# Fourier mixing and a squared-ReLU layer: a cosine table by permutation, another fold order for the first batch, and stores by group at the end

## The chip, the cores and the metric

The kernel runs on one core of a Trainium2 chip. The metric is device time in microseconds (us) of one execution; where one number stands for several executions it is their median. The profiled execution is one of its own, with a time of its own.

## What is computed

The reference, cut to what matters (x is 8 x 3008 x 256, w_in 256 x 2048, w_out 2048 x 256, all float32):

```python
X = np.fft.fft(np.fft.fft(x, axis=1), axis=2).real      # 3008 along the sequence, 256 along the features
t = X.reshape(24064, 256)
h = np.maximum(t @ w_in, 0.0)
out = (h * h) @ w_out                                   # 24064 x 256, float32
```

## The kernel before

**Method.** Only the real part of the two transforms is wanted, and it falls into cosine and sine products. Write C and S for the tables along the sequence, c and s for those along the features. The kernel computes Z = C x and Z' = S x on TensorE (matmuls in float16) with one column for each of half of the output rows. It multiplies c and s into w_in once, which gives `gh` (`gh_step`, L441 to L447: four pieces of 512 columns, two tables each; ACT, the ScalarE, scales them on the way out of PSUM). `gh` times Z and Z', summed, is t @ w_in for one sequence index k. A third product with the doubled, negated sine part (`gh_turn`, L449) turns this sum in place into that of the mirrored row S − k. So every column of Z serves two output rows.

**Folds.** x is folded before it is multiplied: along d (feature d with 256 − d) and along n (sequence place n with its mirrors), so that the odd frequencies need 752 places and the even ones fewer. For each batch: x comes in as four quarters of its rows, xo, 128 partitions x 6 rows x 256 (`load_x`, L116; plain and indirect DMAs that POOL, the GpSimd, issues and that make float16 of float32). DVE, the VectorE, folds in d (`d_even` L360, `d_odd` L364: 128 x 3072 elements each), then in n (`n_cos` L369, `n_sin` L372), then makes the odd class `od` (`odd` for one half, `odds` for both, L376 and L379) and the even class `ev` (`even`, L390). `nyq` (L381) moves one column of `od` with two permutation matmuls. The even class goes to a scratch DRAM tensor and back in another order (`scr`, `rb`, L392 to L406), and is folded again by `fold8` and `fold16` (L415, L426; the `late` steps). Batch 0 of the fold order is x[1]; x[0] comes last.

**Tables.** `table_steps` (L228) makes the sine and cosine tables by range reduction: `args` and `turns` round, `mods` gives the remainder m, `absm` |m| for the cosine, and ACT's Sin function does the rest (`sins`, `coss`, L270 to L280). For the odd class each table has six rows of 376 columns. `weigh` (L282) halves the rows' end places with the small vector `wgt`, which POOL makes (L202 to L207). The even class's table (e = 1) is made later, in window 2.

**Windows.** The 12,040 columns of Z are cut into 25 windows (`FIRST`, then 512 each; the last has 360). Units (i, e), fold number and class, hold some 752 columns each: (0, 0), (1, 0), (0, 1), (1, 1), then both classes of each batch in turn. Every window has eight stages (L694 to L705), and each stage has two of 16 blocks of 128 hidden features:

- `pq`: four matmuls into PSUM (L666, L667).
- `square`: ReLU on ACT (L676), square on DVE (L678).
- `others`: the fold or table steps of this stage (`at`, `post`), an eighth of the second product of the previous window (`ffn2_steps`, matmuls L587), and from stage `lo` to `hi` the Z products of the units that begin in the next window (`z_steps`, L461).
- `turn`: two matmuls (L672), then `square` again for the mirrored rows.

Window 0 takes its stages in pairs. A Z product of a unit has two parts (0 cosine, 1 sine). Each is made in two halves: the first goes through ACT into `es` (L486), the second stays in PSUM, ACT copies it to `zc` or `zs` (L490), and `minus` (L497) gets the other columns as 2 es − PSUM on DVE.

**Second product.** `part` (L580) sums 16 matmuls for each group of 128 output rows. Two groups share a PSUM tile; then ACT copies both at once into `osb` (L593; in the last window the pieces are 128 x 512 and 128 x 256), and SP, the SyncE, issues the stores (L569), one for each run of rows with an even step.

**What sets the order.** `tc.manual_schedule()` (L98): the program text is the order on each engine. Each engine runs its own queue in order and waits on semaphores for the others. Ahead of window 0, L531 to L552 set it: `weigh`, the folds, the Z products of unit (0, 0), all four `gh_step`s, `minus` (jobs `z0(0, 2)`, `z0(1, 2)`) and all `gh_turn`s. 28 matmuls of zeros on the tile `spn` (L327) stand ahead of these on PE, the TensorE.

The functions that the change touches, and their callers:

Of the kernel before, what the change touches and what calls it, by code (L numbers as in the profile page):

```python
# [14 lines left out]
HS = 32.0  # L15
# [13 lines left out]
def kernel(  # L29
# [136 lines left out]
    evec_i = iota([P, 2], [[1, 2]], 0, 2, "evec_i")  # L166
    dvec_i = iota([P, 2], [[P, 2]], 0, 1, "dvec_i")
    xs = {0: load_x(0, idx_first)}
    w16 = const.tile([P, 2, F], F16, name="w16")
    nc.gpsimd.dma_start(out=w16, in_=moe_w_in.rearrange("(c p) f -> p c f", p=P))  # L170
    wout16 = const.tile([P, NFC, D], F16, name="wout16")
    nc.gpsimd.dma_start(out=wout16, in_=moe_w_out.rearrange("(c p) o -> p c o", p=P))
    prow_i = iota([P, P], [[1, P]], 0, 1, "prow_i")
    idx["c"] = iota([P, 1], [[1, 1]], P - 1, -1, "idx_c")
# [21 lines left out]
    phase = small([P, R], "phase")  # L196
    nc.gpsimd.tensor_scalar(out=phase, in0=nraw, scalar1=0.0, scalar2=float(math.pi / 2), op0=ALU.is_ge, op1=ALU.mult)
    wg0 = small([P, R], "wg0")
    nc.gpsimd.tensor_scalar(out=wg0, in0=nraw, scalar1=float(Q), scalar2=None, op0=ALU.is_le)
    nc.gpsimd.tensor_tensor(phase, phase, wg0, op=ALU.mult)  # L200

    wgt = small([P, R], "wgt")  # L202
    wg1 = small([P, R], "wg1")
    nc.gpsimd.tensor_scalar(out=wgt, in0=nraw, scalar1=0.0, scalar2=-0.5, op0=ALU.is_equal, op1=ALU.mult)
    nc.gpsimd.tensor_scalar(out=wg1, in0=nraw, scalar1=float(Q), scalar2=-0.5, op0=ALU.is_equal, op1=ALU.mult)
    nc.gpsimd.tensor_tensor(wgt, wgt, wg1, op=ALU.add)
    nc.gpsimd.tensor_scalar(out=wgt, in0=wgt, scalar1=1.0, scalar2=None, op0=ALU.add)  # L207


    perm = [const.tile([P, P], F16, name=f"perm{i}") for i in range(2)]  # L210
    for i in range(2):
        nc.gpsimd.tensor_scalar(out=perm[i], in0=prow_i, scalar1=float(P - 1 - i), scalar2=None, op0=ALU.is_equal)
# [15 lines left out]
    def table_steps(e):  # L228
# [44 lines left out]
        def coss(h):  # L273
            if e:
                nc.scalar.activation(cos_t, st["t", h][:, 0:nr, 0:n], AF.Sin, bias=halfpi[:, 0:1], scale=-wk)
                return

            for j0, j1 in ((0, 1), (1, 2), (2, 3)) if h == 0 else ((0, 1), (1, 3)):
                r = RQ[3 * h + j0]
                nc.scalar.activation(cos_t[:, 3 * h + j0 : 3 * h + j1, :], st["t", h][:, j0:j1, 0:n], AF.Sin, bias=phase[:, r : r + 1], scale=-wk)  # L280

        def weigh():  # L282
            if e:
                for t in (cos_t, sin_t):
                    for r in range(2):
                        nc.vector.tensor_scalar(out=t[:, r, :], in0=t[:, r, :], scalar1=wge[:, r : r + 1], scalar2=None, op0=ALU.mult)
                return

            for t, r in ((cos_t, 5), (sin_t, 1)):
                q = RQ.index(r)  # L290
                nc.scalar.activation(t[:, q, :], t[:, q, :], AF.Copy, bias=0.0, scale=wgt[:, r : r + 1])
# [16 lines left out]
    for c in range(2):  # L308
        nc.vector.scalar_tensor_tensor(out=am[:, c, :], in0=drow, scalar=dvec[:, c : c + 1], in1=at[:, c, :], op0=ALU.mult, op1=ALU.add)
    to["args"](0)  # L310
# [10 lines left out]
    spn = fop.tile([P, 2, 2, P], F16, name="spn")  # L321
    to["turns"](0)
    to["mods"](0)
    nc.vector.memset(spn, 0.0)  # L324

    pw = ps_o.tile([P, 512], F32, name="pw", tag="po")
    for i in range(28):  # L327
        nc.tensor.matmul(pw[:, 0 : 3 * P], spn[:, 0, 0, :], spn.rearrange("p c r d -> p (c r d)")[:, 0 : 3 * P], start=True, stop=True)  # L328
    to["absm"](0)
    to["turns"](1)  # L330
    to["sins"](0)
    to["coss"](0)
    to["mods"](1)
    to["absm"](1)
    to["sins"](1)
    to["coss"](1)
    fe = fop.tile([P, 4, R, 130], F16, name="fe")
    fo = fop.tile([P, 4, R, 130], F16, name="fo")
    fo0 = fo.rearrange("p q c d -> p (q c) d")[:, :, 0:1]
    nc.vector.memset(bass.AP(tensor=fo0.tensor, offset=fo0.offset, ap=list(fo0.ap[0:2]) + [[129, 2]]), 0.0)  # L340
    nc.vector.memset(fe.rearrange("p q c d -> p (q c) d")[:, :, 129:130], 0.0)

    folded = {}

    def fold_steps(i):
        t = xs.pop(i)
        ab = fop.tile([P, 2, 2, R, 130], F16, name="ab", tag="ab")
# [7 lines left out]
        fef = fe.rearrange("p q c d -> p (q c) d")  # L355
        fof = fo.rearrange("p q c d -> p (q c) d")
# [17 lines left out]
        def odd(part):  # L374

            nc.vector.tensor_tensor(od[:, part, :, part:129], ab[:, part, 0, :, part:129], ab[:, part, 1, :, part:129], op=ALU.subtract)  # L376

# [10 lines left out]
        def even():  # L388

            nc.vector.tensor_tensor(ev.rearrange("p r c d -> p c r d"), ab[:, :, 0], ab[:, :, 1], op=ALU.add)  # L390
            scr = drp.tile([R * P, 260], F16, name="scr", tag="scr")
            nc.gpsimd.dma_start(out=scr.rearrange("(p r) d -> p (r d)", r=R), in_=ev.rearrange("p r c d -> p (r c d)"))  # L392
            st["scr"] = scr
# [15 lines left out]
        def fold8(sg):  # L409
            if sg == 0:  # L410
                xt = st["xt"] = fop.tile([P, 2, 2, 2, 260], F16, name="xt", tag="xt")
                yt = st["yt"] = fop.tile([P, 2, 2, 2, 130], F16, name="yt", tag="yt")
                folded[i, 1] = (xt, yt)
            rb = st["rb"]
            nc.vector.tensor_tensor(st["xt"][:, sg], rb[:, 0:2], rev_dim(rb[:, 2:4], 2), op=ALU.subtract if sg else ALU.add)  # L415
# [21 lines left out]
        return {"d_even": d_even, "n_cos": n_cos, "odd": odd, "odds": odds, "d_odd": d_odd, "n_sin": n_sin, "nyq": nyq, "even": even, "back": back, "late": late}  # L437
# [3 lines left out]
    def gh_step(cc):  # L441
        f0 = cc * 512
        pg = ps_h.tile([P, 2, 512], F32, name="pg", tag="psh")
        for i, t in enumerate((c_all, s_n)):
            for c in range(2):
                nc.tensor.matmul(pg[:, i, :], t[:, c, 0:P], w16[:, c, f0 : f0 + 512], start=(c == 0), stop=(c == 1))  # L446
        nc.scalar.activation(gh[:, 0:2, f0 : f0 + 512], pg, AF.Copy, bias=0.0, scale=1.0 / HS)  # L447
# [13 lines left out]
    def z_steps(u, late=False):  # L461
# [15 lines left out]
        def mm(part, h, k, last, o0, o1, lhs, tab):  # L477
            if h == 0 and k == 0:
                st[part] = ps_z.tile([P, 512], F32, name="pz", tag="pz")
            ps = st[part]  # L480
            nc.tensor.matmul(ps[:, o0:o1], lhs, tab, start=(h == 0 and k == 0), stop=last, skip_group_check=True)  # L481
            if not last:
                return
            if h == 0:
                es = st["es", part] = evp.tile([P, NE], F32, name="es", tag="es")
                nc.scalar.activation(es[:, 0:n], ps[:, 0:n], AF.Copy, bias=0.0, scale=1.0)  # L486
                return
            es = st["es", part]
            for w, o, a, cnt in spans(c0, n):
                nc.scalar.activation(zwin(w)[part][:, o : o + cnt], ps[:, a : a + cnt], AF.Copy, bias=0.0, scale=1.0)  # L490
            if not late:
                minus(part)

# [5 lines left out]
        def jobs(part, h):  # L499
            if h == 2:  # L500
                return [lambda: minus(part)]
# [25 lines left out]
    def run(*jobs):  # L527
        for j in jobs:
            j()
# [3 lines left out]
    to["weigh"]()  # L533
    run(f0s["d_even"], f0s["n_cos"], lambda: f0s["odd"](0))
    run(*z0(0, 0))
    run(f0s["d_odd"])
    gh_step(0)
    run(*z0(0, 1))
    run(f0s["n_sin"], lambda: f0s["odd"](1), f0s["nyq"])
    gh_step(1)  # L540
    gh_step(2)
    run(*z0(1, 0))
    run(*z0(1, 1))
    gh_step(3)
    run(*z0(0, 2))
    run(*z0(1, 2))

    turn2 = small([P, 1], "turn2")
    nc.vector.tensor_scalar(out=turn2, in0=dvec[:, 0:1], scalar1=0.0, scalar2=2.0, op0=ALU.is_equal, op1=ALU.mult)
    nc.vector.tensor_scalar(out=turn2, in0=turn2, scalar1=-2.0, scalar2=None, op0=ALU.add)  # L550
    for cc in range(F // 512):
        gh_turn(cc)  # L552

    def store(osb, p0, g0, m, minus):

        for b, k0, kstep, n, c0 in runs:
# [12 lines left out]
            nc.sync.dma_start(  # L569
# [3 lines left out]
    def ffn2_steps(w, h2):  # L573
# [6 lines left out]
        def part(i, hf):  # L580
# [7 lines left out]
            if hf == 1 and (j == 1 or i + 1 == len(groups)):  # L588
# [33 lines left out]
    for w in range(NW):  # L622
# [7 lines left out]
        if w == 0:  # L630
            at[2] = [f0s["even"], f0s["back"]]
        elif w == 1:
            fj = fold_jobs(1)
            at = [[f] for f in fj[0:5]] + [[], fj[6:7], []]
            post[5] = fj[5:6]
            lo, hi = 6, NST
        elif w == 2:
            te = table_steps(1)
            at = [[lambda: te["freq"](), lambda: te["args"](0)], [lambda: te["turns"](0)], [lambda: te["mods"](0)],
                  [lambda: te["absm"](0)], [lambda: te["sins"](0)], [lambda: te["coss"](0)], [], [lambda: te["weigh"]()]]  # L640
            for st in range(4):
                at[st + 3] = at[st + 3] + f0s["late"][st : st + 1]
            at[7].append(folds[1]["back"])
# [4 lines left out]
        elif w == win_of(col_of[1, 1]) - 1:  # L648
            for st in range(4):
                at[st] = folds[1]["late"][st : st + 1]  # L650
            lo = 4
# [55 lines left out]
    for j in ffn2_steps(*old):  # L707
        j()
# [30 lines left out]
```

## Time and profile before

| | |
|---|---|
| three runs | 640.37 us median (640.24 to 640.47) |
| the profiled execution | 640.28 us |
| its span in the trace | 638.4 us |
| PE busy | 615.2 us, 96% of the span |
| ACT busy | 459.4 us, 72% |
| DVE busy | 369.8 us, 58% |
| POOL busy | 79.9 us, 13% |
| moved by DMA | 47.52 MB |

PE is the bound, at nearly full load; the matmuls of the second product (L587) alone take 361.7 us. How to read it: the span is what the trace covers from the first to the last instruction, and the execution's own time is 1.9 us longer. Line numbers of the kernel before are written L587. A `window` of the kernel is one of the 25 stretches of columns; it is not a window of time. Times along the span are counted from its start.

### The profile page before, as it was taken

Reading aid. Unit: us, or ns where it says so; the run is one execution under the profiler, and the core shown is the slowest. Engines: PE = TensorE matmul, PEld = TensorE weight load, DVE = VectorE, ACT = ScalarE, POOL = GpSimd, SP = SyncE. Lnnn points to the kernel's source line nnn. Section 1 sums busy time; section 2 is a strip of 40 time slices with the busy share of each in tenths; the row PEclk is TensorE's granted clock in tenths of the full one; section 3 lists DMA queues with packets and bytes.
Section 4 is the critical chain, followed back from the end, with each engine's and each line's share of the span. In section 5 each row is a group of like instructions: output and inputs, shape, how many; then the busy total and the mean of one; then the engine's idle time right before and its main releaser. Section 6 shows DMA issues by size and latency. Waiting matters only on the chain.

```text
span 638.4 us, 11578 instructions
## 1 busy us (share of the span) xinstructions
PE 615.2 (96%) x4540; PEld 438.1 (69%) x4540; DVE 369.8 (58%) x604; ACT 459.4 (72%) x612; POOL 79.9 (13%) x131
## 2 busy tenths in 40 slices
PE   4789999999999999999999999999999999999995
PEld 2456796676776767776677767776777767777785
DVE  8786645775547557745576455854567545454440
ACT  7777767867777777767777777777777777776751
POOL 8450110022001300210011100130000200000000
PEclk9999999999999999999999999999999999999998
DMA  8935121072111711631117211262111311111112
GB/s 161 193 70 130 49 75 42 24 151 90 43 43 43 178 60 51 142 97 36 50 39 169 69 51 39 59 160 61 40 43 50 101 36 48 37 48 49 37 55 57
DMA packets 36268, 47.52 MB, mean 74 GB/s; under 512 B 4215, under 2 KB 30327, under 8 KB 36215
## 3 DMA queue, kind: packets, MB, share of 16 engines
q0 software_dynamic: 9072, 22.14, 17.0%
q1 hardware_dynamic: 27143, 24.65, 12.9%
q8 instruction: 35, 0.57, 0.4%
q14 instruction: 18, 0.15, 0.1%
HBM read 33.63 MB, written 27.84 MB: 96 GB/s over the span
## 4 chain that ended last, share of the span: by engine, by line
PE 90%; ACT 4%; DMA 2%; issue 2%; DVE 1%; POOL 1%; ACTq 0%; POOLq 0%
PE po L587 50%; PE ph L672 13%; PE ph L666 12%; PE ph L667 12%; PE pz L481 3%; ACT h L676 3%; DMA w<-in_moe_w_in_dram 2%; ACT gh L447 1%; DVE h L678 0%; POOL xo L130 0%; PE pg L446 0%; ACT osb L593 0%; DVE od L379 0%; POOL xo L125 0%; ACT zc L490 0%
## 5 line engine op out<-in xcount | busy, mean ns | idle before, releaser
L676 ACT ACTIVATE h<-ph 128x1024 f16<-128x1024 f32 (+3 forms) x400 | 368.4, 974 | 80.8 <-PE ph L672 77.4
L678 DVE TENSOR_TENSOR h<-h 128x1024 f16<-128x1024 f16 (+3 forms) x400 | 262.8, 660 | 233.4 <-ACT h L676 231.6
L587 PE MATMUL po<-wout,h 128*128 128x256 f16 (+1 forms) x3024 | 361.7, 273 | 0.0
L587 PEld LDWEIGHTS <-h 128*128 128x128 f16 (+1 forms) x3024 | 296.6, 98 | 71.5
L666 PE MATMUL ph<-zc,gh 128*128 128x512 f16 (+3 forms) x400 | 145.4, 366 | 1.2 <-ACT gh L447 0.7
L667 PE MATMUL ph<-zs,gh 128*128 128x512 f16 (+3 forms) x400 | 145.5, 366 | 0.1
L672 PE MATMUL ph<-zs,gh 128*128 128x512 f16 (+3 forms) x400 | 113.8, 366 | 4.6 <-ACT h L676 4.2
L593 ACT ACTIVATE osb<-po 128x512 f32<-128x512 f32 (+2 forms) x98 | 56.8, 584 | 68.2 <-PE po L587 63.4
L667 PEld LDWEIGHTS <-gh 128*128 128x128 f16 x400 | 39.1, 98 | 44.9 <-issue 2.8
L666 PEld LDWEIGHTS <-gh 128*128 128x128 f16 x400 | 39.0, 98 | 42.6 <-issue 0.4
L672 PEld LDWEIGHTS <-gh 128*128 128x128 f16 x400 | 37.0, 97 | 14.8 <-issue 8.0
L432 POOL COPY xt<-xt 128x2 f16<-128x2 f16 x16 | 2.5, 187 | 184.4 <-DVE xt L415 184.4
L130 POOL DMA_INDIRECT xo<-in_x_dram,idx_r x15 | 18.8, 1256 | 4.5 <-issue 4.3
L125 POOL DMA_DIRECT2D xo<-in_x_dram x8 | 6.1, 760 | 101.8 <-DVE fo L364 101.7
L402 POOL DMA_INDIRECT rb<-scr,idx_r x16 | 18.1, 1133 | 4.9 <-issue 4.9
L486 ACT ACTIVATE es<-pz 128x376 f32<-128x376 f32 (+1 forms) x32 | 15.4, 481 | 4.3 <-PE pz L481 4.2
L490 ACT ACTIVATE zs<-pz 128x376 f16<-128x376 f32 (+23 forms) x27 | 8.5, 359 | 10.8 <-PE pz L481 10.8
L328 PE MATMUL pw<-spn 128*128 128x384 f16 x28 | 7.3, 444 | 8.2 <-DVE spn L324 8.2
L497 DVE SCALAR_TENSOR_TENSOR zs<-es,pz 128x376 f16<-128x376 f32 (+22 forms) x27 | 9.4, 383 | 9.8 <-ACT zs L490 9.8
L360 DVE TENSOR_TENSOR fe<-xo 128x3072 f16<-128x3072 f16 x8 | 14.3, 1786 | 0.3
L364 DVE TENSOR_TENSOR fo<-xo 128x3072 f16<-128x3072 f16 x8 | 14.2, 1780 | 0.0
L497 DVE SCALAR_TENSOR_TENSOR zc<-es,pz 128x376 f16<-128x376 f32 (+22 forms) x27 | 9.4, 383 | 6.9 <-ACT zc L490 6.9
(108 smaller groups left out, 225.1 us busy)
## 6 DMA issues: line engine op xcount, KB each, us to landing
out_dram<-osb SPq DMA_DIRECT2D x77, 128.0 KB
xo<-in_x_dram POOLq DMA_DIRECT2D x7, 768.0 KB, 7.0
scr<-ev POOLq DMA_DIRECT2D x8, 390.0 KB, 4.1
rb<-scr POOLq DMA_DIRECT2D x16, 130.0 KB, 3.6
out_dram<-osb SPq DMA_DIRECT2D x12, 94.0 KB
w<-in_moe_w_in_dram POOLq DMA_DIRECT2D x1, 1024.0 KB, 11.9
wout<-in_moe_w_out_dram POOLq DMA_DIRECT2D x1, 1024.0 KB, 16.4
out_dram<-osb SPq DMA_DIRECT2D x8, 75.0 KB
```

The costliest lines, as they stand in the source:

```text
L130: nc.gpsimd.indirect_dma_start(out=flat(q), out_offset=None, in_=bass.AP(tensor=x.tensor, offset=0, ap=[[XW, B * S * D // XW], [1, XW]]), ...
L402: nc.gpsimd.indirect_dma_start(out=rb[:, q].rearrange("p r d -> p (r d)"), out_offset=None, in_=bass.AP(tensor=src.tensor, offset=src.offs ...
L481: nc.tensor.matmul(ps[:, o0:o1], lhs, tab, start=(h == 0 and k == 0), stop=last, skip_group_check=True)
L486: nc.scalar.activation(es[:, 0:n], ps[:, 0:n], AF.Copy, bias=0.0, scale=1.0)
L497: nc.vector.scalar_tensor_tensor(out=zwin(w)[part][:, o : o + cnt], in0=es[:, a : a + cnt], scalar=2.0, in1=ps[:, a : a + cnt], op0=ALU.mu ...
L587: nc.tensor.matmul(po[0:m, j * D : (j + 1) * D], h2[:, fc, q : q + m], wout16[:, fc, :], start=(fc == 0), stop=(fc == NFC - 1))
L593: nc.scalar.activation(osb[0:mm].rearrange("p s d -> p (s d)")[:, lo:hi], po[0:mm, lo:hi], AF.Copy, bias=0.0, scale=HS * HS)
L666: nc.tensor.matmul(ph[:, a, 0:wn], gh[:, 0, f0 : f0 + P], zcw[:, 0:wn], start=True, stop=False)
L667: nc.tensor.matmul(ph[:, a, 0:wn], gh[:, 1, f0 : f0 + P], zsw[:, 0:wn], start=False, stop=True)
L672: nc.tensor.matmul(phs[s][:, a, 0:wn], gh[:, 2, f0 : f0 + P], zsw[:, 0:wn], start=False, stop=True, skip_group_check=True)
L676: nc.scalar.activation(h1[:, :, 0:wn], phs[s][:, :, 0:wn], AF.Relu)
L678: nc.vector.tensor_tensor(h2[:, 2 * s : 2 * s + 2, sg * wn : (sg + 1) * wn], hv, hv, op=ALU.mult)
```

## The change

- **Cosine table (odd class).** The six rows of the cosine table are no longer computed by Sin from |m|. Each is a mirror image of a row of the sine table, so two matmuls with permutation matrices (`perm`) put two rows at a time into PSUM, and ACT copies them out (three copies of 128 x 752). `absm` for this table, its two Sin calls for six rows, and the vectors `phase` and `wg0` go; `wgt` shrinks to one column, and one weighing is left. POOL makes `perm` early. The 28 zero matmuls become 16 + 4 + 4 + 8, spread between these steps, and `spn` is cleared earlier.
- **Fold of batch 0.** It is folded in n first, on all 256 features, then in d: `u_odd` and `u_part` make the odd class; `v_even` and `v_part` make the even class later, in window 2. The next load of x is issued after `v_even`.
- **w_in** is loaded by two DMAs of half the columns. `gh` pieces 0 and 1 are made ahead of window 0 (0 scaled by ACT, 1 by DVE), piece 2 in stage 0 (ACT) and piece 3 in stage 2 (DVE) of window 0, into the PSUM tiles of the second product. `minus` of unit (0, 0), with ACT's copies of the columns of window 1 (`rest`), stands in stage 4 of window 0.
- **Windows 1 to 4.** The folds of batch 1, the even class's table, the `late` folds and the Z products are put into other stages.
- **The end.** In the last window each group of rows is copied and stored by itself; the odd groups' mirrored rows are stored through ACT's queue.

The diff, cut to its core:

```diff
-    w16 = const.tile([P, 2, F], F16, name="w16")
-    nc.gpsimd.dma_start(out=w16, in_=moe_w_in.rearrange("(c p) f -> p c f", p=P))
+    w16 = [const.tile([P, 2, F // 2], F16, name=f"w16_{i}") for i in range(2)]
+    for i in range(2):
+        nc.gpsimd.dma_start(out=w16[i], in_=moe_w_in[:, i * F // 2 : (i + 1) * F // 2].rearrange("(c p) f -> p c f", p=P))
...
+    for i in (1, 0):
+        nc.gpsimd.tensor_scalar(out=perm[i], in0=prow_i, scalar1=float(P - 1 - i), scalar2=None, op0=ALU.is_equal)
...
-    phase = small([P, R], "phase")
-    nc.gpsimd.tensor_scalar(out=phase, in0=nraw, scalar1=0.0, scalar2=float(math.pi / 2), op0=ALU.is_ge, op1=ALU.mult)
-    wg0 = small([P, R], "wg0")
-    nc.gpsimd.tensor_scalar(out=wg0, in0=nraw, scalar1=float(Q), scalar2=None, op0=ALU.is_le)
-    nc.gpsimd.tensor_tensor(phase, phase, wg0, op=ALU.mult)
-    wgt = small([P, R], "wgt")
...
+    wgt = small([P, 1], "wgt")
+    nc.gpsimd.tensor_scalar(out=wgt, in0=nraw[:, 1:2], scalar1=float(Q), scalar2=-0.5, op0=ALU.is_equal, op1=ALU.mult)
     nc.gpsimd.tensor_scalar(out=wgt, in0=wgt, scalar1=1.0, scalar2=None, op0=ALU.add)
...
         def coss(h):
...
+            pc = ps_h.tile([P, 2, 512], F32, name="pc", tag="psh")
+            for j in range(2):
+                r = RQ[2 * h + j]
+                nc.tensor.matmul(pc[:, j, 0:n], perm[1 if r else 0], sin_t[:, RQ.index(6 - r if r else 0), :], start=True, stop=True)
+            nc.scalar.activation(cos_t[:, 2 * h : 2 * h + 2, :], pc[:, :, 0:n], AF.Copy, bias=0.0, scale=1.0)
...
     to["turns"](0)
     to["mods"](0)
+    to["sins"](0)
     to["turns"](1)
+    to["weigh"]()
+    idle(4)
     to["coss"](0)
     to["mods"](1)
     to["sins"](1)
+    idle(4)
     to["coss"](1)
+    to["coss"](2)
+    idle(8)
...
+        def u_odd():
+            nc.vector.tensor_copy(t[0:1, 2, 0, :], t[0:1, 0, R - 1, :])
+            nc.vector.tensor_tensor(u, tq[:, :, 0], tq[:, :, 1], op=ALU.subtract)
+        def u_part(sg):
+            nc.vector.tensor_tensor(cs[:, sg], u[:, 0], rev_dim(u[:, 1], 1), op=ALU.subtract if sg else ALU.add)
+            d_fold(od[:, sg], cs[:, sg], sg)
+            if not sg:
+                nc.scalar.activation(od[:, 0, :, 0:1], cs[:, 0, :, 0:1], AF.Copy, bias=0.0, scale=1.0)
+        def v_even():
+            nc.vector.tensor_tensor(v, tq[:, :, 0], tq[:, :, 1], op=ALU.add)
+            xs[i + 1] = load_x(i + 1)
+        def v_part(sg):
+            w = fop.tile([P, R, D], F16, name="w", tag="ab")
+            nc.vector.tensor_tensor(w, v[:, 0], rev_dim(v[:, 1], 1), op=ALU.subtract if sg else ALU.add)
+            d_fold(ev[:, :, sg], w, sg)
...
+    def gh_scale(out, pg, act):
+        if act:
+            nc.scalar.activation(out, pg, AF.Copy, bias=0.0, scale=1.0 / HS)
+        else:
+            nc.vector.tensor_scalar(out=out, in0=pg, scalar1=1.0 / HS, scalar2=None, op0=ALU.mult)
+    def gh_step(cc, act, late=False):
...
+        pg = None if late else ps_h.tile([P, 2, 512], F32, name="pg", tag="psh")
+            pt = ps_o.tile([P, 512], F32, name="pg", tag="po") if late else pg[:, i, :]
...
+                if late and w > 0:
+                    continue
                 nc.scalar.activation(zwin(w)[part][:, o : o + cnt], ps[:, a : a + cnt], AF.Copy, bias=0.0, scale=1.0)
...
+        def rest(part):
+            for w, o, a, cnt in spans(c0, n):
+                if w > 0:
+                    nc.scalar.activation(zwin(w)[part][:, o : o + cnt], st[part][:, a : a + cnt], AF.Copy, bias=0.0, scale=1.0)
...
-                return [lambda: minus(part)]
+                return [lambda: minus(part), lambda: rest(part)]
...
-    to["weigh"]()
-    run(f0s["d_even"], f0s["n_cos"], lambda: f0s["odd"](0))
-    run(*z0(0, 0))
-    run(f0s["d_odd"])
-    gh_step(0)
-    run(*z0(0, 1))
-    run(f0s["n_sin"], lambda: f0s["odd"](1), f0s["nyq"])
-    gh_step(1)
-    gh_step(2)
-    run(*z0(1, 0))
-    run(*z0(1, 1))
-    gh_step(3)
-    run(*z0(0, 2))
-    run(*z0(1, 2))
-    for cc in range(F // 512):
-        gh_turn(cc)
+    run(f0s["u_odd"], lambda: f0s["u_part"](0))
+    run(*z0(0, 0))
+    gh_step(0, True)
+    run(lambda: f0s["u_part"](1), f0s["nyq"])
+    run(*z0(0, 1))
+    gh_step(1, False)
+    run(*z0(1, 0))
+    run(*z0(1, 1))
+    gh_turn(0)
+    gh_turn(1)
+    run(f0s["v_even"])
...
+            if hf == 1 and tail:
+                osb = osp.tile([P, 2, D], F32, name="osb", tag="osb")
+                nc.scalar.activation(osb[0:m, 0, :], po[0:m, j * D : (j + 1) * D], AF.Copy, bias=0.0, scale=HS * HS)
+                nu = max(0, min(m, wn - q))
+                if nu:
+                    store(osb[:, 0, :], 0, g0 + q, nu, False)
+                if nu < m:
+                    store(osb[:, 0, :], nu, g0 + 2 * wn - q - m, m - nu, True, nc.scalar if i % 2 else nc.sync)
...
         if w == 0:
-            at[2] = [f0s["even"], f0s["back"]]
+            at[0] = [lambda: gh_step(2, True, True), lambda: gh_turn(2)]
+            at[2] = [lambda: gh_step(3, False, True), lambda: gh_turn(3)]
+            at[4] = z0(0, 2) + z0(1, 2)
         elif w == 1:
-            at = [[f] for f in fj[0:5]] + [[], fj[6:7], []]
+            at = [[], fj[0:1], fj[1:2], fj[2:3], fj[3:5], [], [], []]
...
         elif w == 2:
...
-            at[7].append(folds[1]["back"])
+            at = [[folds[1]["even"]], [lambda: te["freq"](), lambda: te["args"](0)], [lambda: f0s["v_part"](0)], [lambda: f0s["v_part"](1), f0s["even"], f0s["back"]],
+                  [lambda: te["turns"](0)], [lambda: te["mods"](0)], [lambda: te["absm"](0), lambda: te["sins"](0)], [lambda: te["coss"](0)]]
+        elif w == 3:
+            at[0] = [lambda: te["weigh"]()]
+            for st in range(4):
+                at[1 + st // 2] = at[1 + st // 2] + f0s["late"][st : st + 1]
+            at[3] = [folds[1]["back"]]
+            lo, hi = 4, NST
...
         elif w == win_of(col_of[1, 1]) - 1:
             for st in range(4):
-                at[st] = folds[1]["late"][st : st + 1]
-            lo = 4
+                at[1 + st] = folds[1]["late"][st : st + 1]
+            lo, hi = 5, NST
...
-    for j in ffn2_steps(*old):
+    for j in ffn2_steps(*old, tail=True):
```

In the prediction, L561, L736 and L741 are lines of the changed kernel: L561 is the subtraction in `minus` (L497 before), L736 the second matmul of `pq` (L667 before) and L741 that of `turn` (L672 before).

## The prediction

> **What bounds the kernel now.** I read the 40 slices first, then the chain of waits of the first 60 us, then the timeline of each engine there and at the end.
>
> ```profile
> PE   4789999999999999999999999999999999999995
> PE 90%; ACT 4%; DMA 2%; issue 2%; DVE 1%; POOL 1%; ACTq 0%; POOLq 0%
> ```
>
> TensorE (PE) is full from slice 4 on and holds 90% of the chain. The change takes no matmul out of that part, so time can only be won or lost before PE is full (the first 55 us), where one window hands over to the next, and after the last matmul. Table by stage (us, then PE, PEld, DVE, ACT, POOL busy; the last row is the hand-over from window 3 to 4, where PE lacks 1.1 us):
>
> ```profile
> 15.00:20.00 5.00, 4.05 (x23) 1.84 (x22) 4.90 (x7) 2.25 (x5) 4.59 (x6) 1.00 1.32 197
> 20.00:25.00 5.00, 3.24 (x21) 1.84 (x19) 1.96 (x8) 3.96 (x7) 2.65 (x3) 1.00 1.19 182
> 30.00:35.00 5.00, 4.26 (x28) 2.51 (x26) 3.17 (x8) 4.36 (x8) 1.49 (x4) 1.00 0.29 101
> 100.00:110.00 10.00, 8.89 (x56) 5.27 (x55) 6.14 (x11) 7.95 (x10) 0.31 (x2) 1.00 0.08 26
> ```
>
> The chain there (start, us, what):
>
> ```profile
> 5.26 11.87 DMA w<-in_moe_w_in_dram
> 17.17 1.04 PE pg L446 x4
> 18.23 1.02 ACT gh L447
> 19.70 1.87 ACT gh L447 x2
> 21.99 0.64 PE pz L481 x3
> 23.53 1.03 ACT gh L447
> ```
>
> Window 0 waits for w_in and then for ScalarE (ACT), which copies four gh pieces between the z copies. Its first ReLU starts at 24.45, window 1's first matmul at 33.10 and window 2's at 55.31. The end:
>
> ```profile
> 628.64 4.38 SPq L569 DMA_DIRECT2D out_dram<-osb  x8
> 631.56 0.65 ACT L593 ACTIVATE osb<-po 128x256 f32<-128x256 f32 x2 [2.95 <-PE po L587]
> SPq L734 <- DMA out_dram<-osb: 3.4, 1, 3.4
> ```
>
> The last matmul ends at 631.49, the last store is issued by 633.02, SP then waits 3.4 us for stores to land (636.5), and 1.9 us close the span at 638.4. The profiled execution took 640.28 against a median of 640.37 (640.24 to 640.47), so I add to 640.28.
>
> **Part 1, up to window 0's first ReLU: 3.4 us earlier.** GpSimd (POOL) now makes both perms before wgt. By starts in its timeline, L197, L199, L200, L205 and L206 go (0.72 + 0.33 + 0.45 + 0.32 + 0.59 = 2.41), two perms (1.56) and one more DMA issue (0.74) come: wgt, 11.10 before, is ready at 11.0. ACT, in its new order, waits there: weigh 0.50, a cosine copy of 752 columns from PSUM (no such row: 0.60 for 512 and 1.02 for 1024 bound it, I take 0.80), the second sine 1.14 (no longer at 11.54 but at 12.3), 0.4 for the permutation matmuls, two copies 1.5, one od column 0.2: 15.5. So the permutations do not bring the cosine forward: it was done at 14.5, and is now done at 15.3. VectorE (DVE) has x at 12.15 (issued 4.24, 7.9 to land) and needs 1.79 + 0.96 + 0.57: od at 15.5 as well. The first z matmul starts at 15.5 instead of 16.43.
>
> From there the two sides differ more. od's second part is ready at 16.9, not 19.67; the first half of w_in should land near 14.7 (it follows x in the same queue: half of the 17.13 − 12.15); gh 1 is scaled by DVE (about 1.2 for 1024 columns from PSUM, from the 0.55 that 376 take at L497) and gh 2 and 3 are gone from here. In order on ACT: es 16.2, gh 0 17.1 to 18.1, zc to 18.5, es to 19.4; PE's last z block 19.5 to 20.1; zs 20.1 to 20.5; the first products; ReLU at **21.0**.
>
> **Part 2, window 0 itself: 3.2 us longer.** It now holds what was ahead of it. Pair 0 (stages 0 and 1): two gh copies on ACT, 2 x 0.52, of which 0.8 are on the path. Pair 1: four gh matmuls (0.87) stand on PE ahead of the turning matmuls that ACT waits for: 0.5. Pair 2: the subtractions (0.55 each) and ACT's copies into window 1 are queued here, and the built program's waits say that each copy waits for its subtraction. On DVE these stand behind the square of the pair's second ReLU, on ACT the copies stand ahead of the next ReLUs. So from the end of that ReLU (near 28.2) ACT waits for a square (0.39) and two subtractions, overlapped by 0.08, and makes the second copy (0.28): it goes on at 29.9, and PE's pair 3 and window 1 stand behind it: 1.7, with some 0.2 for hand-overs **1.9**. Two gh scalings on DVE (0.68 each by the slope above) and gh_turn 0.29 end before that ReLU does, at 27.3, and v_even (1.79) delays pair 0's squares alone; three h1 buffers cover both. Window 0 thus takes 8.65 + 3.2, and window 1 starts at 32.8 instead of 33.10: −0.3.
>
> The next x load is issued after v_even, near 22 instead of 19.81, and lands by 32.5 (8.5 as in its row); window 1 folds it from about 38, so this costs nothing while 5 us of cover hold.
>
> **Part 3, windows 1 to 5: +1.9.** Window 1 folds one stage later and puts n_sin and the odd fold (0.97 each) in one stage. DVE then has no gap from 5.4 us into the window on (seven fold operations 6.9, six squares 4.1, less 0.6 of overlap): od is ready at 15.8 instead of 14.2, and PE reaches the Nyquist matmuls that need it after 14.8: 0.5 of that is not covered by the wait for ReLU that follows anyway. In window 2, ev of batch 1 (0.96) and both v_parts (3.2) replace the late folds (2.2) on a DVE that is busy 70%: nothing. Batch 0's scratch store and gathers go from 29.7 to 38.7 to about 69 to 80; they are wanted near 84, some 4 us of cover; without it, DVE and the squares behind it wait.
>
> z of unit (0, 1) now ends in window 3's last stage, not its seventh. Window 4's sine products then wait for ACT's osb (0.60), zs (0.49) and DVE's 135 columns (0.30), less what PE still has to do: 0.9, with nothing there before. Window 4 to 5 likewise, where a wait of 0.39 stands already: 0.5 more. From then on PE is full.
>
> **Part 4, the end: −0.7.** With one eviction for each group, two groups still share a PSUM bank, and by the list of waits the odd group's first matmul waits for the even group's copy: 0.17 from matmul to copy, 0.38 the copy, 0.06 back: 0.61, three times, **+1.8** on a PE that had no wait there (96 matmuls in 10.49). Against that, group 4's stores leave 2.4 us earlier seen from PE's end, and only one store of 80 rows is left after it: copy 0.45, issue, 0.85 until data flows (628.64 to 629.5, as at 621.35), under 1 us of data. Landing was 5.0 after PE's end. The new one lies between 1.8 (nothing else under way) and 4.3 (only the last issue comes sooner, by 0.7); I take 2.5, so **−2.5**, nearer the short end, since 80 rows are left after PE where there were 208. How far the old stores had spread shows here:
>
> ```profile
> 633.00:633.50 0.50, 0.00 (x0) 0.00 (x0) 0.00 (x0) 0.00 (x0) 0.00 (x0) 1.00 0.38 55
> 636.00:636.50 0.50, 0.00 (x0) 0.00 (x0) 0.00 (x0) 0.00 (x0) 0.00 (x0) 0.50 0.08 29
> ```
>
> A share of 0.08 is one or two of 16 DMA engines. The Trainium skill (DMA: Bandwidth & Descriptors, "Why a DMA increments its semaphore by 16 and not by 1") says that a store runs on the largest number of engines up to 16 that divides its rows, counted from the lowest. By that rule 94, 58, 69 and 92 rows use 2, 2, 3 and 4 engines, the lowest one gets some 130 rows of the last two pairs, and storing by group would end its queue about 2 us after PE, an estimate that would make the end 0.5 better than mine.
>
> **Sum:** −0.3 + 0.5 + 0.9 + 0.5 − 0.7 = +0.9, so **641.2**.
>
> **Rivals.**
> 1. Faster: the waits of the last groups are not paid. If the copy of a group is done by the time that PE has loaded the next weights, the 1.8 goes: 639.4, and 638.7 with the shortest landing. It decides from a hand-over of about one matmul (0.11) on. For it: PE passes from pair to pair with no wait now. Against: those pairs lie in two banks; here the wait is written down, and the copy alone takes 0.38.
> 2. Slower: wgt is late. Tiny POOL operations take 0.24 to 0.50 until 11 us, but 0.97 to 1.83 after 12.9, when DVE folds in f16. If the new perms and wgt run at the slow price, wgt comes 2 us later, and the second sine, the cosine and the first matmul with it: 643.2. It decides from 0.3 on, where ACT and DVE are level. Against: DVE does the same f32 work beside them as it did.
> 3. Slower: PE falls back to its starting pace. The warm-up matmuls start 0.32 apart for 5.1 us and then 0.167, with PEclk at 9 throughout; a gap of 1.06 at 21 us changed nothing. The new order has gaps of about 1.5 at 12.5 and 2.0 in pair 2. If half pace follows, 2.17 of matmuls in a stage of 2.62 become 4.3, and window 1's first two stages lose 1.7 each: 644.6. The Trainium skill (TensorE: Matmul & The Clock Gate, "What's actually happening") puts the fall-back at an idle window of about 3.4 us; by that nothing is lost, and no row here has so long a gap.
> 4. The end gives nothing: the last store lands as long after PE as before, less only its shorter issue (0.7): 643.0.
> 5. The change does not do what it says for the cosine (above); this is in the sum.
>
> **Chances.** Forecast 0.58 (640.0 to 642.6, each term off by a fifth or so), rival 1 0.10, rival 2 0.10, rival 3 0.06, rival 4 0.16. What a measurement of this kernel can tell from no change is about 0.2%, 1.3 us, so "same" is 639.0 to 641.6. Of the forecast 0.35 lie there, 0.17 above and 0.06 below (a faster start than I see); of rival 1 half below, half within; rivals 2 to 4 above. Faster 0.11, same 0.40, slower 0.49. The range leaves out rival 3, half of rival 1 and the forecast's lowest part, 0.15: 639.2 to 643.4.
>
> **What would show it.** Right: first z matmul near 15.5, first ReLU of window 0 near 21.0, window 1's first matmul near 32.8 with ACT standing behind L561 in pair 2 for over 1 us, a wait of L741 or L736 of about 0.9 at window 4's start, three waits of 0.6 in the last six groups, and SP's last wait well under 3.4. Wrong: a first ReLU after 22, a window 0 under 10 us, or a PE that waits in the last six groups for less than 1 us in all.

## The result, and the profile after

The changed kernel takes 641.52 us (median of 13 runs, 641.38 to 642.62) beside 640.46 (640.15 to 641.91) for the kernel before: a ratio of 1.0018, 95% interval 1.0010 to 1.0027. It is 1.1 us slower; 641.2 was forecast. The profiled execution took 641.41, its span is 639.4.

Single runs of most kernels here are 0.5 to 1.6 us longer than the others of the same kernel, at a granted clock lower by 0.002 to 0.005; this matters for one number below (the first experiment's).

Where the time went, by the start of each window's first matmul (L666 before, L735 after):

| us | before | after | difference | forecast |
|---|---|---|---|---|
| first Z matmul | 16.43 | 15.72 | −0.7 | −0.9 |
| window 0, first ReLU | 24.45 | 21.26 | −3.2 | −3.4 |
| window 1 | 33.10 | 33.02 | −0.1 | −0.3 |
| window 2 | 55.31 | 56.48 | +1.2 | +0.2 |
| window 4 | 100.01 | 101.18 | +1.2 | |
| window 5 | 121.00 | 123.29 | +2.3 | +1.1 |
| window 6 | 144.10 | 146.64 | +2.5 | +1.6 |
| window 24 | 599.53 | 602.07 | +2.5 | +1.6 |
| TensorE's last matmul ends | 631.47 | 635.95 | +4.5 | +3.4 |
| span | 638.44 | 639.39 | +0.9 | +0.9 |

From window 6 to window 24 the two kernels run in step to 0.01. The page after, TensorE's line and its granted clock in 40 slices, then the chain by engine:

```profile
PE   5699998999999999999999999999999999999996
PEclk9989999999999999999999999999999999999999
PE 89%; ACT 4%; DVE 2%; issue 2%; POOL 1%; DMA 1%; SPq 0%; ACTq 0%; POOLq 0%; DVEq 0%
```

TensorE is full one slice earlier, but slice 7 (96 to 112 us, window 4) has a dent, and in slice 3 (32 to 48 us) the clock is lower. VectorE has 2% of the chain, where it had 1%. The same stretches as before the change (PE, PEld, DVE, ACT, POOL busy, clock, DMA share, GB/s):

```profile
15.00:20.00 5.00, 4.29 (x26) 2.08 (x25) 3.53 (x6) 2.85 (x6) 0.53 (x2) 1.00 1.30 202
20.00:25.00 5.00, 3.76 (x28) 2.60 (x27) 3.91 (x9) 3.92 (x9) 2.03 (x3) 1.00 0.91 110
30.00:35.00 5.00, 4.02 (x18) 2.03 (x18) 2.63 (x8) 3.28 (x8) 0.00 (x0) 0.71 0.49 95
100.00:110.00 10.00, 8.47 (x59) 5.27 (x57) 5.23 (x10) 6.34 (x8) 0.00 (x0) 1.00 0.08 27
```

From 30 to 35 TensorE is busy 4.02 with 18 matmuls where it did 28 in 4.26: nearly the same busy time, fewer matmuls, a clock of 0.71. The chain of waits there (start, us, what) shows what came before:

```profile
28.47 0.41 DVE h L747
28.88 0.46 DVE zc L561
29.34 0.47 DVE zs L561
29.80 0.02 issue
29.83 0.02 ACT zs L556
29.85 0.07 issue
29.94 0.07 issue
30.01 0.57 ACT h L745
30.58 0.04 issue
30.62 0.26 PE ph L735
```

After a square, two subtractions stand on VectorE, ScalarE's copies (L556, `rest`) wait for them, its next ReLU (30.01) stands behind the copies, and TensorE does nothing from 28.86 to 30.62. TensorE's and SyncE's waits at the end, and the last stretches with DMA:

```profile
PE po L642 <- ACT osb L646: 1.5, 3, 0.5
```

```profile
SPq L803 <- DMA out_dram<-osb: 3.2, 2, 2.9
```

```profile
637.00:637.50 0.50, 0.00 (x0) 0.00 (x0) 0.00 (x0) 0.00 (x0) 0.00 (x0) 1.00 0.48 143
637.50:638.00 0.50, 0.00 (x0) 0.00 (x0) 0.00 (x0) 0.00 (x0) 0.00 (x0) 1.00 0.15 49
```

There are three new waits of TensorE. SyncE's wait fell only from 3.4 to 3.2, but it starts earlier, seen from TensorE: the span ends 3.44 after the last matmul, where it was 6.97.

### The profile page after: what moved, and what is told of

Its sections match the earlier page's. It is cut to its first block, busy times and chain, and to the rows that moved or that the text cites. A ratio compares the mean times of both kernels' runs of the same rounds, so it can differ in the third digit from the quotient of the medians.

```text
span 639.4 us, 11588 instructions
## 1 busy us (share of the span) xinstructions
PE 617.4 (97%) x4550; PEld 439.0 (69%) x4550; DVE 371.7 (58%) x608; ACT 456.9 (71%) x611; POOL 75.5 (12%) x130
## 4 chain that ended last, share of the span: by engine, by line
PE 89%; ACT 4%; DVE 2%; issue 2%; POOL 1%; DMA 1%; SPq 0%; ACTq 0%; POOLq 0%; DVEq 0%
PE po L642 49%; PE ph L741 12%; PE ph L736 12%; PE ph L735 12%; PE pz L538 4%; ACT h L745 2%; DVE h L747 1%; DMA out_dram<-osb 1%; ACT cos L275 0%; POOL xo L130 0%; DVE fe L408 0%; ACT osb L657 0%; PE pg L500 0%; POOL w L170 0%; DVE fo L412 0%
## 5 line engine op out<-in xcount | busy, mean ns | idle before, releaser
L735 PE MATMUL ph<-zc,gh 128*128 128x512 f16 (+3 forms) x400 | 145.9, 367 | 3.5 <-ACT h L745 3.1
L736 PE MATMUL ph<-zs,gh 128*128 128x512 f16 (+3 forms) x400 | 145.9, 368 | 1.3 <-DVE zs L561 0.7
L741 PE MATMUL ph<-zs,gh 128*128 128x512 f16 (+3 forms) x400 | 113.7, 367 | 3.5 <-ACT h L745 3.2
L657 ACT ACTIVATE osb<-po 128x512 f32<-128x512 f32 (+2 forms) x94 | 54.9, 586 | 59.6 <-PE po L642 54.0
L736 PEld LDWEIGHTS <-gh 128*128 128x128 f16 x400 | 39.1, 98 | 47.1 <-issue 3.2
L735 PEld LDWEIGHTS <-gh 128*128 128x128 f16 x400 | 39.1, 98 | 44.4 <-issue 2.6
L741 PEld LDWEIGHTS <-gh 128*128 128x128 f16 x400 | 37.1, 98 | 13.6 <-issue 6.2
L478 POOL COPY xy<-xy 128x2 f16<-128x2 f16 x16 | 2.5, 188 | 165.4 <-DVE xy L461 165.4
L549 ACT ACTIVATE zs<-pz 128x376 f16<-128x376 f32 (+22 forms) x26 | 8.3, 362 | 9.7 <-PE pz L538 9.7
L561 DVE SCALAR_TENSOR_TENSOR zc<-es,pz 128x376 f16<-128x376 f32 (+22 forms) x27 | 9.4, 384 | 7.3 <-ACT zc L549 7.3
L561 DVE SCALAR_TENSOR_TENSOR zs<-es,pz 128x376 f16<-128x376 f32 (+22 forms) x27 | 9.4, 383 | 7.1 <-ACT zs L549 7.1
L437 POOL DMA_DIRECT2D scr<-ev x8 | 4.7, 593 | 70.0 <-DVE ev L435 63.0
L538 PE MATMUL pz<-sin,od 128*128 128x376 f16 x48 | 12.2, 322 | 0.6 <-ACT es L543 0.6
L408 DVE TENSOR_TENSOR fe<-xo 128x3072 f16<-128x3072 f16 x7 | 12.5, 1786 | 0.2
```

The lines of the kernel that those rows point to most:

```text
L561: nc.vector.scalar_tensor_tensor(out=zwin(w)[part][:, o : o + cnt], in0=es[:, a : a + cnt], scalar=2.0, in1=ps[:, a : a + cnt], op0=ALU.mu ...
L657: nc.scalar.activation(osb[0:mm].rearrange("p s d -> p (s d)")[:, lo:hi], po[0:mm, lo:hi], AF.Copy, bias=0.0, scale=HS * HS)
L735: nc.tensor.matmul(ph[:, a, 0:wn], gh[:, 0, f0 : f0 + P], zcw[:, 0:wn], start=True, stop=False)
L736: nc.tensor.matmul(ph[:, a, 0:wn], gh[:, 1, f0 : f0 + P], zsw[:, 0:wn], start=False, stop=True)
L741: nc.tensor.matmul(phs[s][:, a, 0:wn], gh[:, 2, f0 : f0 + P], zsw[:, 0:wn], start=False, stop=True, skip_group_check=True)
```

## The experiments

My theory was the forecast's sum, with one term new from the trace: the drop in clock. The rivals stand with each run. Effects in us are differences of medians.

**1 and 2. The end alone, from both sides.** First the changed kernel with the old end:

```diff
-    for j in ffn2_steps(*old, tail=True):
+    for j in ffn2_steps(*old):
```

> The changed kernel, but the last window's groups are copied and stored in pairs, all through SP, as before the change. Theory (the end is worth its own sum: TensorE loses 1.9 to three waits for the copy, landing after TensorE's last matmul falls from 6.9 to 3.5): without it TensorE ends 1.9 earlier and the stores land 3.4 later, so 641.5 + 1.5 = 643.0. Rival (the earlier landing is a matter of this one profiled run or of when TensorE ends, the waits are real): 641.5 - 1.9 = 639.6. Everything ahead of the last window should stay as in the changed kernel, window 24 starting at 602.1.

Measured: 643.62 (642.73 to 643.93), ratio to before 1.0050 (1.0036 to 1.0064). Two runs lie at 642.7 to 642.8 with a clock of 0.996 and 0.995, three at 643.6 to 643.9 with 0.991, so the median is 0.6 above the theory and the faster runs 0.2 below; the rival (639.6) is out. Then the kernel before with the new `part` and `store` and `tail=True`:

> The kernel before, with the change's last window alone (one copy and own stores for each group, odd groups' mirrored rows through ScalarE's queue). Theory: 640.4 + 1.9 (three waits of TensorE) - 3.4 (landing) = 638.9. Rival (the end gains nothing by itself): 642.3 with the waits paid and the landing as long as before. The first profile up to window 24 should be that of the kernel before, window 24 starting at 599.5.

Measured: 638.91, ratio 0.9976 (0.9967 to 0.9985), as the theory has it. The same line of waits is there (L591 is the new copy in that kernel):

```profile
PE po L587 <- ACT osb L591: 1.5, 3, 0.5
```

So the end is a gain of 1.5 by itself, and all that is ahead of it is a loss of 2.5.

**3. The clock.** In window 0, behind the turning matmuls of stages 4 and 5:

```diff
+            if w == 0 and s0 == 4:
+                pw = ps_o.tile([P, 512], F32, name="pw", tag="po")
+                idle(9, pw)
```

> The changed kernel with nine matmuls of zeros (384 columns) put into TensorE's gap of 1.77 us in window 0, behind the turning matmuls of stages 4 and 5; no wait is taken away. Theory (the half clock that the profile shows from 32.06 to 35.47 comes from that gap, and costs 0.4 in window 0's last turn and some 0.8 in window 1's first stage): PEclk stays at 1.00 there, window 1's first two stages take 2.6 each as in the kernel before, window 2 starts 0.8 to 1.2 earlier, 640.3 to 640.7. Rival (ScalarE's ReLUs bound these stages anyway): PEclk at 1.00, but 641.5. Second rival (the drop has another cause): PEclk 0.50 there again, 641.5.

Measured: 640.43, ratio 1.0006 (0.9997 to 1.0015). Window 1 starts at 32.88, window 2 at 55.49, 1.0 earlier than in the changed kernel. Its rows and then those of the changed kernel:

```profile
28.50:30.50 2.00, 1.76 (x11) 1.01 (x11) 1.24 (x3) 1.01 (x4) 0.00 (x0) 1.00 1.02 199
32.00:35.50 3.50, 2.97 (x19) 1.66 (x18) 2.15 (x7) 2.31 (x4) 0.00 (x0) 1.00 0.07 13
```

```profile
28.50:30.50 2.00, 0.35 (x2) 0.18 (x2) 1.29 (x3) 0.96 (x4) 0.00 (x0) 1.00 1.08 212
32.00:35.50 3.50, 3.40 (x12) 1.53 (x12) 1.70 (x6) 2.04 (x4) 0.00 (x0) 0.51 0.09 17
```

The zeros take away none of the work that TensorE waits for (the first product behind the gap starts at 30.57, in the changed kernel at 30.62); they only keep it busy in its gap (1.76 of 2.00 instead of 0.35). With them the clock stays at 1.00, and from 32.0 to 35.5 TensorE gets through 19 matmuls, not 12. So the gap costs its own length and 1.0 more, some three us later.

**4. The copy first.**

```diff
-                return [lambda: minus(part), lambda: rest(part)]
+                return [lambda: rest(part), lambda: minus(part)]
```

> The changed kernel with one pair of steps turned round: in window 0's stage 4 ScalarE's copy of the columns of window 1 is issued ahead of VectorE's subtraction, so that the subtraction waits for the copy and not the copy for the subtraction. Theory (the 3.1 us that window 0 lost are mostly ScalarE standing in its queue behind VectorE in pair 2): TensorE's gap of 1.77 falls to about 0.4, window 1 starts 1.5 to 2.0 earlier (near 31.2), and with the gap the half clock goes too (another 0.8 to 1.2): 638.3 to 639.2. Rival (the subtractions stand ahead of the squares on VectorE, and the squares hold the h1 buffers, so the wait only moves there): window 1 near 32.5, 640.5 to 641.5.

Measured: 639.12, ratio 0.9981 (0.9972 to 0.9990). Window 1 starts at 31.57 (−1.45), the clock stays at 1.00, window 2 at 54.19 (−2.3). TensorE's waits for the ReLUs ahead of `pq` until 40 us were 3.1 in the changed kernel, 1.8 the longest; here:

```profile
PE ph L735 <- ACT h L745: 2.0, 4, 0.9
```

One reordered pair of steps takes 2.4 us off. The next four runs start from this kernel (639.12).

**5. The Z stages of windows 3 and 4 as before the change**, and with them the `late` folds of window 4, which share its stages:

```diff
-            lo, hi = 4, NST
+            lo, hi = 3, NST - 1
...
-                at[1 + st] = folds[1]["late"][st : st + 1]
-            lo, hi = 5, NST
+                at[st] = folds[1]["late"][st : st + 1]
+            lo = 4
```

> The changed kernel with the copy first (as in the run before, 639.1), and the Z products of window 3 in stages 3 to 6 instead of 4 to 7, those of window 4 in stages 4 to 6 and its late folds in stages 0 to 3, as before the change. Theory (windows 4 and 5 lose 1.12 and 0.25 because their first products wait for copies and subtractions of a Z product that ends in the stage ahead of them): the waits of L736 for zs (0.7) and L735 for zc (0.2) go, window 5 starts 1.1 earlier and window 6 another 0.2 to 0.3: 637.7. Rival (the products then stand closer behind the late folds on VectorE and wait there instead): 638.5 to 639.1.

Measured: 637.76, ratio 0.9964 (0.9951 to 0.9978). Window 5 starts 1.10 earlier, window 6 1.33. The changed kernel had these two waits between 40 and 130 us, and both are gone here:

```profile
PE ph L736 <- DVE zs L561: 0.7, 1, 0.7
...
PE ph L735 <- ACT zc L549: 0.2, 1, 0.2
```

**6. The fold stages of window 1 as before the change.**

```diff
-            at = [[], fj[0:1], fj[1:2], fj[2:3], fj[3:5], [], [], []]
+            at = [[f] for f in fj[0:5]] + [[], [], []]
```

> The changed kernel with the copy first (639.1), and window 1's fold of batch 1 in stages 0 to 4, one operation each, as before the change. Theory (window 1 loses 0.4 to 0.6 because od comes late for the Nyquist matmuls, since the fold starts a stage later and two operations share the last one): the wait of L428 (0.6) goes, window 2 starts 0.4 to 0.6 earlier: 638.6. Rival (x of batch 1 is loaded later than before and is not there in stage 0, so VectorE stands and with it the squares): 639.1 to 640.5.

Measured: 638.67, ratio 0.9974 (0.9964 to 0.9984); window 2 starts 0.39 earlier. The wait of the Nyquist matmul (`nyq`) for od (0.6) is gone, and it is worth 0.45 in time.

**7. A PSUM tile for each group in the last window.**

```diff
-            if j == 0 and hf == 0:
+            if (tail or j == 0) and hf == 0:
```

> The changed kernel with the copy first (639.1), and in the last window a PSUM tile of its own for each group instead of one for two. Theory (TensorE waits three times because the odd group's first matmul goes into the bank that ScalarE is still reading): the three waits of 0.47 to 0.52 go, with the drain of three groups 1.9 in all, and landing after TensorE's end stays at 3.5: 637.2. Rival (the stores are then what ends last, since groups follow each other every 1.75 where a group's stores take longer to land): landing 4.5 or more, 638.2 or more.

Measured: 638.19, ratio 0.9970 (0.9960 to 0.9980). Both theories are half right: TensorE's three waits are gone and it ends 1.9 earlier (631.79, not 633.67), but the span ends 4.3 later than that, not 3.4. The stretches after its last matmul:

```profile
633.00:633.50 0.50, 0.00 (x0) 0.00 (x0) 0.00 (x0) 0.00 (x0) 0.00 (x0) 1.00 0.61 193
633.50:634.00 0.50, 0.00 (x0) 0.00 (x0) 0.00 (x0) 0.00 (x0) 0.00 (x0) 1.00 0.16 55
634.00:634.50 0.50, 0.00 (x0) 0.00 (x0) 0.00 (x0) 0.00 (x0) 0.00 (x0) 0.98 0.11 37
```

After the peak, which fits the last store of 80 rows, shares of 0.16 and 0.11 go on for 1 us: two or three engines of 16 still work off something.

**8. The cosine table as before the change**, with `phase`, `wg0`, the six columns of `wgt`, and the zero matmuls in one block:

```diff
-    idle(16)
...
+    idle(28)
+    to["absm"](0)
...
+    to["absm"](1)
...
-                nc.tensor.matmul(pc[:, j, 0:n], perm[1 if r else 0], sin_t[:, RQ.index(6 - r if r else 0), :], start=True, stop=True)
-            nc.scalar.activation(cos_t[:, 2 * h : 2 * h + 2, :], pc[:, :, 0:n], AF.Copy, bias=0.0, scale=1.0)
+                nc.scalar.activation(cos_t[:, 3 * h + j0 : 3 * h + j1, :], st["t", h][:, j0:j1, 0:n], AF.Sin, bias=phase[:, r : r + 1], scale=-wk)
```

> The changed kernel with the copy first (639.1), and the cosine table as before the change: from |m| by six rows of Sin, with phase, wg0 and six columns of wgt on GpSimd, permutation matrices after them, 28 zero matmuls in one block. Theory (the permutations do not bring the first Z matmul forward, since x's landing at 12.2 and 3.3 of VectorE bound it as well; VectorE only has the |m| of the second half ahead of the fold): first Z matmul 0.2 to 0.5 later than 15.72, 639.3 to 639.6. Rival (freeing ScalarE of Sin, VectorE of |m| and GpSimd of the phase vector is what brings the start forward): first Z matmul at 16.7 or later, 640.1 or more.

Measured: 639.63, ratio 0.9989 (0.9980 to 0.9998): 0.5 slower, just past the theory's range; the first Z matmul starts at 16.31. VectorE's timeline there (L272 is |m|, L392 `u_odd`):

```profile
11.67 0.94 DVE L272 TENSOR_SCALAR t<-m 128x1128 int32<-128x1128 int32 x1
12.53 0.25 DVE L391 COPY xo<-xo 1x256 f16<-1x256 f16 x1
12.81 1.76 DVE L392 TENSOR_TENSOR u<-xo 128x3072 f16<-128x3072 f16 x1
```

The tables themselves are ready at 15.2 here and at 15.5 with permutations. What the permutations bring is VectorE: without |m| it starts on x at 12.2, when x lands, and not at 12.8.

**9 to 12.** The four edits of runs 4 to 7 together:

> The changed kernel with the four single edits together: the copy first, the Z stages of windows 3 and 4 and the fold stages of window 1 as before the change, and a PSUM tile for each group in the last window. Theory (each was a wait of its own on TensorE, so they add up): 639.12 - 1.36 - 0.45 - 0.93 = 636.4. Rival (where one wait goes, the next one behind it comes up, ScalarE's ReLUs in window 1 and the Nyquist matmuls above all): 637.0 or more.

Measured: 636.35, ratio 0.9946 (0.9932 to 0.9960). They add up. Then each store of the last three groups is cut into a multiple of 16 rows and a rest, which goes through the other queue:

```diff
+            cut = cnt // 16 * 16 if split else cnt
+            for k, (a, n1) in enumerate(((0, cut), (cut, cnt - cut))):
+                if n1:
+                    (other if k else eng).dma_start(
...
```

> As the four edits together, and each store of the last three groups cut into a multiple of 16 rows and a rest (58 = 48 + 10, 69 = 64 + 5, 92 = 80 + 12, 36 = 32 + 4), the rest issued through the other of ScalarE's and SyncE's queues. Theory (with a bank for each group the stores end 4.3 after TensorE instead of 3.4, because stores of 58, 69 and 92 rows go through few DMA engines, as the shares of 0.16 and 0.11 at the end show): 0.9 less than the four edits together, 635.5. Rival (the number of stores or the last store's own path of issue and landing is what ends late): 636.4, or up to 0.8 more for the added issues.

Measured: 635.17, ratio 0.9928 (0.9914 to 0.9942), 1.2 less. The stretch from 632.0 to 632.5, which still carried 41 GB/s in run 9 (first line), is empty here (the other two), with the same last matmul to 0.05:

```profile
632.00:632.50 0.50, 0.00 (x0) 0.00 (x0) 0.00 (x0) 0.00 (x0) 0.00 (x0) 1.00 0.12 41
...
631.50:632.00 0.50, 0.00 (x0) 0.00 (x0) 0.00 (x0) 0.00 (x0) 0.00 (x0) 1.00 0.14 43
632.00:632.50 0.50, 0.00 (x0) 0.00 (x0) 0.00 (x0) 0.00 (x0) 0.00 (x0) 1.00 0.00 0
```

The single transfers in the traces (packets) point to the reason. Beside a packet of 1 KB for each row, the queues carry packets of 4 bytes. ScalarE's queue, which is used in the last window alone, has 228 packets in run 9: 207 for its stores of 58, 69 and 80 rows, and 21 of 4 bytes, which is 2 + 3 + 16, the largest divisors up to 16 of these numbers. In run 10 it has 272: 208 for pieces of 48, 64, 80, 12 and 4 rows, and 64 of 4 bytes, 16 + 16 + 16 + 12 + 4. Of the 16 that belong to the last store of run 9, fourteen stand by 631.62, the other two at 632.36 and 632.62; in run 10 all 16 stand between 631.44 and 631.68. SyncE's store of 92 rows, which has four of them, is under way until 632.41 in run 9. So two of the sixteen parts of the last store end 1 us late, which fits a place behind the earlier stores of few parts, and cutting by 16 rows takes that away.

From run 4's kernel, with w_in in one DMA:

```diff
-    for i in range(2):
-        nc.gpsimd.dma_start(out=w16[i], in_=moe_w_in[:, i * F // 2 : (i + 1) * F // 2].rearrange("(c p) f -> p c f", p=P))
+    nc.gpsimd.dma_start(out=w16, in_=moe_w_in.rearrange("(c p) f -> p c f", p=P))
```

> The changed kernel with the copy first (639.1), and w_in loaded by one DMA as before the change. Theory (the first half lands ahead of 16.2, the whole at about 17.1 as before, and everything from the first gh matmuls on waits for it): the first gh matmul at 17.1 instead of 16.21, window 0 0.9 later, 640.0. Rival (the first ReLU of window 0 waits for Z and ScalarE and not for gh): 639.1 to 639.4.

Measured: 640.21, ratio 0.9994 (0.9985 to 1.0003): 1.1 slower than run 4. TensorE waits until 17.20 for what it needs at 16.4:

```profile
PE pg L499 <- DMA w<-in_moe_w_in_dram: 0.8, 1, 0.8
```

Last, from run 10's kernel:

```diff
-            at[0] = [lambda: gh_step(2, True, True), lambda: gh_turn(2)]
+            at[0] = [lambda: gh_step(2, False, True), lambda: gh_turn(2)]
```

> As the kernel with rows by 16 (635.2), and gh piece 2 in stage 0 of window 0 scaled by VectorE, not by ScalarE. Theory (the 0.97 that ScalarE takes for it stand ahead of the pair's second ReLUs, and TensorE's wait of 0.9 at pair 1 is theirs; VectorE has the room): the wait falls to about 0.2, window 1 starts 0.5 to 0.9 earlier, 634.3 to 634.7. Rival (VectorE gets the 1.2 of scaling ahead of the squares that free the h1 buffers, so ScalarE waits for it in pair 1): 635.0 to 635.7.

Measured: 634.95, ratio 0.9914 (0.9901 to 0.9928), 0.2 less than run 10, which its trace does not show (spans of 633.11 and 633.08). The theory is out, and the time lies at the edge of the rival's range: the wait ahead of `pq` falls from 2.0 to 1.5 (the longest from 0.9 to 0.5), but window 1 starts at 31.53 after 31.55. Of the rival's mechanism only one wait of ScalarE for a square shows (0.2); more of the wait moves to the turning matmuls, whose waits for ScalarE go from 1.4 to 1.7. This is the best version here, 0.9% faster than the kernel before.

## Why the prediction was right, and where it was not

The time, the sign and the likeliest case held (641.2 against 641.5). Of its terms:

- **Part 1 (−3.4): −3.2.** Right in its steps: wgt at 11.24, the first z copy, the first ReLU at 21.26 for 21.0. Run 8 shows that the permutations do not bring the cosine forward. It also shows what the prediction did not say, though its sum had it: without |m| VectorE's fold starts 0.6 earlier, and that is worth 0.5. w_in in halves is worth 1.1 (run 11). The rest of the 3.2, the second part of od at 17.0 and two gh pieces fewer, is read from the trace; no run tried it alone.
- **Part 2 (+3.2): +3.1.** Right, with the mechanism: run 4 takes 1.45 of it away by turning round the two steps of which one waits for the other; 1.9 was forecast for that wait, 1.77 is the gap in the trace. Not all of it comes back, since a wait of 0.9 for ScalarE in pair 1 stays.
- **Part 3 (0.5 + 0.9 + 0.5): 1.25 + 1.12 + 0.25.** Window 1's 0.5 for the late od was 0.45 (run 6). The rest of its 1.25 is the step that failed: the prediction left the clock out of the sum and gave it to rival 3, at two stages of 1.7 each and 6 in 100. It happened, behind the gap that the rival named, and cost 1.0 (run 3; 0.14 of it still in window 0). The Z hand-overs came to 1.37 for 1.4 forecast (1.33 by run 5), with more in the first.
- **Part 4 (−0.7): −1.6.** TensorE's +1.8 was +1.9. The mis-sized term is the landing: −2.5 was taken, −3.5 measured. The forecast had the last store land 2.5 after TensorE, 1.8 at the shortest, with nothing else under way. That shortest case came: the last packets of the changed kernel end at 637.7, 1.75 after TensorE, and all earlier stores had ended by 637.34, before the last one. Another 0.2 lies behind the last packet, from which the span ran on for 1.9 before the change and 1.7 after it. With its three waits gone (run 7) TensorE ends 1.9 sooner, the earlier stores are still under way, and the end comes 4.3 after it; by runs 9 and 10 that is a matter of the rows of each store. The Trainium skill (DMA: Bandwidth & Descriptors, "Why a DMA increments its semaphore by 16 and not by 1") has a store run on the largest number of engines up to 16 that divides its rows; the counts of packets in runs 9 and 10 agree with it. By that rule the forecast's own estimate was an end 0.5 earlier than the one taken, and 1.0 came.

The two misses, +1.0 for the clock and −1.0 for the landing, cancel. So the number is better than its working, and that is luck. Rivals 1, 2 and 4 are out: the waits are paid, wgt was in time, and the end did give something. Of rival 3 one part in three came, 1.0 of 3.4: the half pace lasted 3.41 us and not two stages of double length.

Three slips changed nothing: the last matmul of the kernel before ends at 631.47, not 631.49; two of the tiny GpSimd operations after 12.9 take 0.54 and 0.48, under the 0.97 given; and the parts that the range leaves out add up to 0.17, not 0.15.

## What to carry to other kernels

When a step is queued on two engines, look at which of the two waits for the other, and let the engine go first whose next step the bottleneck waits for: here that was ScalarE with its ReLUs, and the order of two steps was worth 2.4 us. A gap on TensorE can cost twice, once as a wait and once in clock some us later (1.77 and 1.0 us here); zeros in it bring the second part back. At the end of a kernel, waits and landing pull against each other, so after taking away a wait look at what the DMA engines still have to do, and at how many rows each store has.

## What the hardware showed that I had not expected

The clock fell to 0.50 at 32.06 and came back at 35.47, while TensorE was busy 3.31 of these 3.41 us. The stretches of one clock in this trace last 23.89, 3.41 and 604.16 us, which is 7, 1 and 177 times 3.413, so the traces can be read in windows of that length, counted from where the clock changes. The window ahead of the fall:

```profile
28.65:32.06 3.41, 1.39 (x12) 0.95 (x11) 2.13 (x6) 2.26 (x6) 0.00 (x0) 1.00 1.06 208
```

TensorE worked 1.39 of 3.41, 41%, with no gap longer than 1.77. In run 10 the last window with matmuls and what follows it look like this:

```profile
628.40:631.82 3.42, 1.53 (x15) 1.27 (x12) 0.00 (x0) 0.59 (x2) 0.00 (x0) 1.00 0.31 90
631.82:633.11 1.29, 0.00 (x0) 0.00 (x0) 0.00 (x0) 0.00 (x0) 0.00 (x0) 1.00 0.00 0
```

It was busy 45%, did nothing for the last 1.88, and the clock stayed at 1.00. In the 14 traces every window of 41% or less at full clock, ten of them with some matmuls, most at the end of a run, was followed by 0.50; none of 45% or more was, among them 46% (run 9, 11.47 to 14.88) and 49% (the changed kernel, 11.58 to 14.99). So in these traces the share of a window decides and not the length of one gap, and the limit lies between 41 and 45%, as far as busy times with modelled ends can tell. The Trainium skill (TensorE: Matmul & The Clock Gate, "What's actually happening") gives the free-running window as 3413 ns, which agrees with the 3.41 here; that it takes a whole idle window to fall back does not agree with this trace.
